# Earlier weights, a first gate one step sooner, and one group's x through GpSimd's queue

## The chip, the cores and the metric

The kernel runs on one core of a Trainium2 chip. The metric is the device time of one execution in microseconds; for each kernel the median of several executions is taken. A profile of one execution gives the instructions of each engine with their times: TensorE (PE, with its weight loads PEld), VectorE (DVE), ScalarE (ACT), GpSimd (POOL) and SyncE (SP), which issues most of the DMA transfers.

## What is computed

A gated linear attention runs over 768 positions for 4 batches of 8 heads (head dimension 48); its output, as 3072 rows of 384, goes through a multiplicative feed-forward network.

```python
for t in range(S):
    state = alpha[:, :, t, :, None] * state + np.einsum('bhd,bhe->bhde', k[:, :, t], v[:, :, t])
    y[:, :, t] = np.einsum('bhd,bhde->bhe', q[:, :, t], state)
x = y.transpose(0, 2, 1, 3).reshape(B * S, H * D)   # 3072 x 384
a = x @ w1                                          # 384 x 1024
b = x @ w2                                          # 384 x 1024
h = a * b @ w3                                      # 1024 x 1024
out = h @ w_out                                     # 1024 x 384
```

The four inputs of the attention are float32. The four weights are float64, and the kernel reads them as pairs of 32-bit words and makes float32 of them itself.

## The kernel before

The attention is cut into 24 chunks of 128 positions, six for each batch, and step n of the loop at L577 deals with chunk n. A step has these parts: `scores(n)` (k times q for each head, L344, masked by VectorE at L347), `transposed(n + 1)` (the next chunk's q and k turned by TensorE, L304, and copied by ScalarE, L306), `attend(n - 1)` (the masked scores times v, L370, with the part that comes from the state, L364, ahead of it in `attend_state`), `outer(n)` (the chunk's own contribution to the state, L316, added by VectorE at L324 or L326), `decayed(n + 2)` (q and k multiplied by their decays, L282), `logs(n + 4)` (L251) and `decays(n + 3)` (sums of logarithms by a matmul, L266 or L269, and two exponentials, L272 and L273).

For every even chunk that isn't the first of its batch, the state has to be scaled by a decay over two chunks. Its factors lie in single rows, across partitions where they are needed along them, so they go through memory: GpSimd's queue stores a row of alpha (L258) and two rows of exponentials (L277, L275) into `ends`, reads them back as columns into `dec` (L290), multiplies them (L333, L334) and scales the state (L335). L335's result is read by VectorE at L326 and by TensorE at L364.

The output of a chunk, x, is copied out of PSUM by ScalarE (L374, two copies) and stored by two DMA transfers into `xd[g]`, where g = n // 3 is the group of three chunks. The transfers are put on the list `later`, and the next step's `store()` (L241) issues them on SP's queue. When a group is complete, `load_x(g)` (L386) loads it as `xT`, and `split_x` splits it into three parts for float32-accurate products: ScalarE takes a rounded part (L392), VectorE two remainders (L393, L394).

The feed-forward network begins inside this loop. `begin` says at which step a group is loaded; two steps later it is split, and its gates (a tile of 128 columns of a and of b) are put on the list `fill`. In each step `run` takes so many pieces from this list as `pieces` says: 0, 3, 3, 2 in turn. A piece is one factor of one tile: nine matmuls at L400, then L409 and L411, and after the second factor the product of the two (L448).

The gates need w1 and w2 in float32. They are converted in twelve units of 128 x 512 elements (`load_gates`). A unit begins with two transfers of 256 KB of raw words (L183); then come four portions of work, one for each call of `convert(1)`: L191, L192, L195 and L196; then L198, L199 and L201; then L209; then L211 and L212. The first six units serve the first four tiles, three units for two tiles each. At most three units are under way at once, and `rawp` has three buffers. `fetch` begins units without doing any of their portions.

On each engine and each queue the instructions run in order. That order isn't always the order of the program: the tile framework orders instructions by its own estimate of when they are ready. What follows the loop (the other gates, w3 folded with w_out, the last projection) is mostly TensorE's work at L400.

Of the kernel before, what the change touches and what calls it, by code (L numbers as in the profile page):

```python
# [48 lines left out]
def kernel(  # L49
# [12 lines left out]
    nc = tc.nc  # L62
    B, H, S, D = q.shape
    C = 128
# [5 lines left out]
    DP = 64  # L70
    KM = DM // C
    KF = DF // C
# [46 lines left out]
    def rows(src, n):  # L119
        b, c = divmod(n, NCH)  # L120
        return src[b, :, ds(c * C, C), :].rearrange("h p d -> p h d")

    def load_a(n):
        if n < N:
            st["a", n] = inp.tile([C, H, D], FP32, tag="ac", name="ac")
            nc.sync.dma_start(out=st["a", n], in_=rows(alpha, n))

    def load_kq(n):
        if n >= N:
            return  # L130
        st["kq", n] = inp.tile([C, 2, H, D], FP32, tag="kq", name="kq")
        nc.sync.dma_start(out=st["kq", n][:, 0], in_=rows(k, n))
        nc.sync.dma_start(out=st["kq", n][:, 1], in_=rows(q, n))

    def load_v(n):
        if n < N:
            st["v", n] = vs[n % len(vs)]
            nc.sync.dma_start(out=st["v", n][:, :, 0:D], in_=rows(v, n))
# [77 lines left out]
    def fetch(ahead=3):  # L216
        while weights and len(begun) < ahead:
            begun.append(weights.popleft())
            next(begun[-1])

    def convert(steps, ahead=3):

        for _ in range(steps):
            fetch(ahead)
            if not begun:
                return
            x = begun.popleft()
            try:
                next(x)
                begun.appendleft(x)  # L230
            except StopIteration:
                pass


    later = deque()

    def store():

        while later:
            dst, src = later.popleft()  # L240
            nc.sync.dma_start(out=dst, in_=src)  # L241
# [18 lines left out]
    def decays(n):  # L260
        if n >= N:
            return
        lc = bank()[:, 0:DM]
        la = st.pop(("la", n))
        if n < LATE:
            nc.tensor.matmul(lc, utri if n % 2 else after, la, start=True, stop=True)  # L266
        else:
            for i in range(2):
                nc.tensor.matmul(lc, sums[:, n % 2], la[:, i], start=(i == 0), stop=(i == 1))  # L269

        e = st["e", n] = work.tile([C, 2, DM], FP32, tag="e", name="e", bufs=3)
        nc.scalar.activation(e[:, 0], lc, AF.Exp, scale=-1.0)  # L272
        nc.scalar.activation(e[:, 1], lc, AF.Exp)  # L273
        if n in ends:
            nc.gpsimd.dma_start(out=ends[n][0:1], in_=e[0:1, 0])  # L275
        if n + 1 in ends:
            nc.gpsimd.dma_start(out=ends[n + 1][1:2], in_=e[C - 1:C, 1])  # L277
        load_ends(n)

    def decayed(n):  # L280
        if n < N:
            nc.vector.tensor_mul(qks[n % 3][:, :, :, 0:D], st.pop(("kq", n)),  # L282
                                 st.pop(("e", n)).rearrange("p i (h d) -> p i h d", h=H))
# [69 lines left out]
    def attend_state(n):  # L353
        qkT = st.pop(("qkT", n))

        y = [bank()[:, 0:HP * C].rearrange("p (j c) -> p j c", c=C) for _ in range(2)]
        st["y", n] = y, [(half * HP + j, i, y[i][ds(DP * half, DP), j, :])
                         for j in range(HP) for i in range(2) for half in range(2)]  # L360
        if n % NCH:
            for j, i, to in st["y", n][1]:
                r = ds(DP * i, D)
                nc.tensor.matmul(to, Ts[n % 2][r, j, :], qkT[r, 1, j, :],  # L364
                                 start=(j % HP == 0), stop=False, skip_group_check=True)

    def attend(n):
        (y, heads), ms, vc = st.pop(("y", n)), st.pop(("ms", n)), st.pop(("v", n))
        for j, i, to in heads:
            nc.tensor.matmul(to, vc[:, 2 * j + i, :], ms[:, i, j, :], start=(n % NCH == 0 and j % HP == 0),  # L370
                             stop=(j % HP == HP - 1), skip_group_check=True)
        x = work.tile([C, HP, 2, C], FP32, tag="x", name="x")
        for i in range(2):
            copied = nc.scalar.copy(x[:, :, i], y[i])  # L374
        ends_of_part1[1] = copied.ins
        x = x.rearrange("p j i t -> p (j i) t")

        g, c = divmod(n, G)
        to = xd[g].rearrange("(b h d) t -> b d h t", b=2, d=D)
        for half in range(2):  # L380
            later.append((to[half, :, :, ds(c * C, C)], x[ds(DP * half, D)]))


    def load_x(g, queue=nc.sync):
        st["xT", g] = xp.tile([C, KM, TG], FP32, tag="xT", name="xT")
        queue.dma_start(out=st["xT", g], in_=xd[g].rearrange("(k p) t -> p k t", p=C))  # L386
# [82 lines left out]
    def gate(g, f):  # L469
        yield from (late_gate if late else early_gate)(g, f)  # L470
# [83 lines left out]
    FH = CW // C  # L554
# [7 lines left out]
    transposed(0)  # L562
    logs(1)
    decays(1)
    convert(1, 1)
    load_v(1)
    load_kq(2)
    load_a(3)
    decayed(1)
    load_v(2)  # L570
    load_kq(3)
    load_a(4)


    begin = {4 + 4 * g: (g, range(FH if g < 4 else KF)) for g in range(5)}

    for n in range(N + 1):  # L577
        store()
        load_v(n + AHEAD - 1)
        load_a(n + 5)  # L580
        load_kq(n + AHEAD)
        if n:
            attend_state(n - 1)
        if n < N:
            scores(n)
        transposed(n + 1)
        if n - 2 in begin:
            g, tiles = begin[n - 2]
            split_x(g, 0)
            fill.extend(gate(g, f) for f in tiles)  # L590
        pieces = (0, 3, 3, 2)[(n - 6) % 4] if n > 5 else 0
        if n == 0:
            logs(2)
            decays(2)
            logs(3)
        early = n < 7
        if n < N - 2:
            convert(1, 2 if n == 0 else 3)
        advance(n)
        if n:  # L600
            attend(n - 1)
        outer(n)
        run(pieces > 0)
        if early:
            convert(1)
        decayed(n + 2)
        logs(n + 4)
        if n in begin:
            load_x(begin[n][0])
        convert(early and n > 2)  # L610
        run(pieces > 1)
        decays(n + 3)
        if n < N - 2:
            convert(early or n % 3 == 0)
        run(pieces > 2)
        if n == N - 3:
            while begun:
                convert(1)
            weights.extend(load_out(j) for j in range(KF))
            fetch()  # L620
# [91 lines left out]
```

## Time and profile before

| | us |
|---|---|
| median of 11 executions | 485.95 |
| lowest and highest | 484.06 and 489.77 |
| the profiled execution | 483.23 |
| its span | 481.4 |
| TensorE, mean granted clock | 0.992 |

The profiled execution is a little faster than the median, and its span, from the first to the last instruction, leaves out 1.8 us around it. All waits and durations below belong to this one execution. A few groups of instructions from the page, with the busy time, the mean duration of one, and the idle time of the engine just before them:

```profile
L400 PE MATMUL bank<-x,w 128*128 128x384 f32 x1152 | 211.1, 338 | 0.4 <-DVE x L394 0.4
L282 DVE TENSOR_TENSOR qk<-kq,e 128x768 f32<-128x768 f32 x24 | 22.9, 952 | 9.4 <-ACT e L273 7.3
L347 DVE TENSOR_TENSOR ms<-bank,keep 128x512 int32<-128x512 int32 x48 | 31.1, 683 | 1.3 <-PE bank L344 1.3
L196 ACT ACTIVATE power<-power,rebias 128x512 uint32<-128x512 uint32 (+1 forms) x36 | 25.1, 698 | 15.6 <-DVE power L195 15.6
```

The durations of matmuls overlap, since they are pipelined: 338 ns is not the distance of one from the next. The same holds, to a smaller degree, for VectorE. The page's DMA issues that matter for the start:

```profile
xT<-xd SPq DMA_DIRECT2D x14, 576.0 KB, 4.2
raw<-in_moe_w_dram SPq DMA_DIRECT2D x24, 256.0 KB, 4.7
xd<-x SPq DMA_DIRECT2D x48, 96.0 KB, 3.9
ends<-e POOLq DMA_DIRECT2D x16, 1.5 KB, 3.7
dec<-ends POOLq DMA_DIRECT2D x16, 2.2 KB, 5.0
```

The last column is the median time from issue to landing.

### The profile page before, as it was taken

The numbers are of one execution on the slowest core, as the hardware profiler recorded it, in microseconds if no ns is written. First come the engines' busy times: TensorE is split into PE (matmuls) and PEld (weight loads), VectorE is DVE, ScalarE is ACT, GpSimd is POOL, SyncE is SP. The second block draws the span as 40 slices with busy tenths as digits, with TensorE's granted clock in tenths as the row PEclk, the third lists the DMA queues.
The fourth block names the chain that finished last, engine by engine and source line by source line (L and its number), as shares of the span: only waits on it lengthen the run. The fifth ranks groups of instructions, "written<-read, shape, count | busy, mean of one in ns | idle before, by whom it ended". The sixth has DMA issues, their size and how long they took to land.

```text
span 481.4 us, 9979 instructions
## 1 busy us (share of the span) xinstructions
PE 452.4 (94%) x3824; PEld 429.9 (89%) x3824; DVE 358.5 (74%) x582; ACT 277.4 (58%) x550; POOL 36.5 (8%) x83
## 2 busy tenths in 40 slices
PE   3779679999998999999999998999999999999997
PEld 1557469899898989999999997999999999999996
DVE  2769899997989676999977896884456366667671
ACT  2667667876767544888765665656446333333330
POOL 2122122112202200000000000000000000000000
PEclk9988999999999999999999999999999999999999
DMA  9989999999999954656773353320219455555511
GB/s 170 190 177 219 215 211 205 230 211 248 186 219 222 215 157 124 204 159 216 238 242 96 112 180 114 100 83 34 98 57 266 143 160 169 170 175 177 180 50 50
DMA packets 161295, 80.29 MB, mean 167 GB/s; under 512 B 104672, under 2 KB 155104, under 8 KB 161248
## 3 DMA queue, kind: packets, MB, share of 16 engines
q1 hardware_dynamic: 159968, 79.58, 65.8%
q8 instruction: 30, 0.49, 0.4%
q0 software_dynamic: 1280, 0.08, 0.4%
q14 instruction: 17, 0.14, 0.1%
HBM read 57.58 MB, written 22.06 MB: 165 GB/s over the span
## 4 chain that ended last, share of the span: by engine, by line
PE 75%; DVE 9%; DMA 7%; ACT 3%; issue 2%; SPq 2%; POOL 0%; DVEq 0%; POOLq 0%; ACTq 0%
PE bank L400 63%; PE bank L344 3%; PE bank L370 3%; DMA raw<-in_moe_w_dram 3%; PE bank L304 1%; PE bank L364 1%; DMA dec<-ends 1%; DVE ms L347 1%; DMA ac<-in_alpha_dram 1%; PE bank L502 1%; DVE qk L282 1%; PE bank L316 1%; DMA xd<-x 1%; DMA ends<-e 1%; DVE x L394 1%
## 5 line engine op out<-in xcount | busy, mean ns | idle before, releaser
L400 PE MATMUL bank<-x,w 128*128 128x384 f32 x1152 | 211.1, 338 | 0.4 <-DVE x L394 0.4
L400 PEld LDWEIGHTS bank<-x,w 128*128 128x128 f32 x1152 | 199.9, 188 | 2.8 <-issue 1.4
L400 PE MATMUL bank<-w3o,ab 128*128 128x384 f32 x576 | 100.2, 336 | 0.0
L400 PEld LDWEIGHTS bank<-w3o,ab 128*128 128x128 f32 x576 | 99.9, 188 | 0.0
L425 ACT ACTIVATE bank<-bank 128x384 f32<-128x384 f32 x98 | 46.7, 478 | 36.0 <-PE bank L400 35.7
L409 ACT ACTIVATE t<-bank 128x384 f32<-128x384 f32 x62 | 30.4, 491 | 63.6 <-PE bank L400 63.4
L461 DVE TENSOR_TENSOR ab<-bank,r 128x384 f32<-128x384 f32 x45 | 24.9, 554 | 23.3 <-ACT bank L425 11.5
L531 DVE TENSOR_TENSOR ab<-abl,ab 128x1024 fp32r<-128x1024 f32 x24 | 29.4, 1224 | 13.5 <-ACT ab L530 13.5
L400 PE MATMUL bank<-wo,w3T 128*128 128x384 f32 x192 | 36.3, 335 | 1.9 <-DVE w3T L505 1.1
L530 ACT ACTIVATE ab<-abl 128x1024 fp32r<-128x1024 f32 x24 | 25.5, 1061 | 20.0 <-PE bank L400 18.8
L400 PEld LDWEIGHTS bank<-wo,w3T 128*128 128x128 f32 x192 | 33.4, 188 | 2.5 <-DVE w3T L505 1.4
L344 PEld LDWEIGHTS bank<-qkT 48*128 48x128 f32 x384 | 25.0, 199 | 10.6 <-ACT qkT L306 3.8
L196 ACT ACTIVATE power<-power,rebias 128x512 uint32<-128x512 uint32 (+1 forms) x36 | 25.1, 698 | 15.6 <-DVE power L195 15.6
L306 ACT COPY qkT<-bank 128x512 f32<-128x512 f32 x48 | 25.9, 586 | 14.0 <-PE bank L304 13.9
L411 DVE SCALAR_TENSOR_TENSOR o<-bank,t 128x384 f32<-128x384 f32 x24 | 13.4, 558 | 27.4 <-issue 15.3
L344 PE MATMUL bank<-qkT 48*128 48x128 f32 x384 | 29.7, 297 | 4.3 <-ACT qkT L306 2.6
L191 ACT ACTIVATE rest<-raw 128x512 f32<-128x512 uint32 (+1 forms) x36 | 23.3, 646 | 16.7 <-DMA raw<-in_moe_w_dram 16.6
L347 DVE TENSOR_TENSOR ms<-bank,keep 128x512 int32<-128x512 int32 x48 | 31.1, 683 | 1.3 <-PE bank L344 1.3
L282 DVE TENSOR_TENSOR qk<-kq,e 128x768 f32<-128x768 f32 x24 | 22.9, 952 | 9.4 <-ACT e L273 7.3
L532 DVE SCALAR_TENSOR_TENSOR ab<-ab,abl 128x1024 fp32r<-128x1024 f32 x24 | 29.2, 1218 | 0.0
L411 DVE SCALAR_TENSOR_TENSOR r<-bank,t 128x384 f32<-128x384 f32 x38 | 21.0, 553 | 10.8 <-PE bank L400 7.1
L370 PE MATMUL bank<-ms,v 128*64 128x128 f32 x384 | 27.1, 285 | 0.0
(73 smaller groups left out, 530.6 us busy)
## 6 DMA issues: line engine op xcount, KB each, us to landing
abd<-ab SPq DMA_DIRECT2D x64, 192.0 KB, 2.7
abl<-abd SPq DMA_DIRECT2D x24, 512.0 KB, 4.6
raw<-in_moe_w_dram SPq DMA_DIRECT2D x16, 512.0 KB, 4.5
xT<-xd SPq DMA_DIRECT2D x14, 576.0 KB, 4.2
raw<-in_moe_w_dram SPq DMA_DIRECT2D x24, 256.0 KB, 4.7
ac<-in_alpha_dram SPq DMA_DIRECT2D x24, 192.0 KB, 5.0
kq<-in_k_dram SPq DMA_DIRECT2D x24, 192.0 KB, 5.0
kq<-in_q_dram SPq DMA_DIRECT2D x24, 192.0 KB, 4.5
```

What stands on the lines that cost most here:

```text
L282: nc.vector.tensor_mul(qks[n % 3][:, :, :, 0:D], st.pop(("kq", n)), st.pop(("e", n)).rearrange("p i (h d) -> p i h d", h=H))
L306: nc.scalar.copy(qkT[:, :, :, ds(DP * half, DP)], tp[half])
L344: nc.tensor.matmul(sc[i][:, j, :], qkT[r, 0, j, :], qkT[r, 1, j, :], start=True, stop=True)
L347: masked = nc.vector.tensor_tensor(ms[:, i].bitcast(I32), sc[i].bitcast(I32), keep_bc, op=ALU.bitwise_and)
L370: nc.tensor.matmul(to, vc[:, 2 * j + i, :], ms[:, i, j, :], start=(n % NCH == 0 and j % HP == 0), stop=(j % HP == HP - 1), skip_group_chec ...
L400: nc.tensor.matmul(p, w[part][i], x[part][i], start=start and part == parts[0] and i == 0, stop=stop and part == parts[-1] and i == n - 1, ...
L409: nc.scalar.activation(t, p1, AF.Copy, scale=(1.0 + 1.0 / P) * scale)
L411: nc.vector.scalar_tensor_tensor(to, p2, scale, t, op0=ALU.mult, op1=ALU.add)
L425: nc.scalar.activation(p, p, AF.Copy, scale=1.0 + 1.0 / P)
L530: nc.scalar.activation(t[:, 0], ab, AF.Copy, scale=1.0 - 2.0 ** -13)
L531: nc.vector.tensor_sub(t[:, 1], ab, t[:, 0].bitcast(FP32))
L532: nc.vector.scalar_tensor_tensor(t[:, 2], t[:, 0].bitcast(FP32), -1.0 - 1.0 / P, ab, op0=ALU.mult, op1=ALU.add)
```

## The change

There are four edits, all of them in the part that runs the attention.

1. Ahead of the loop, the raw words of three units are fetched instead of one, between the input loads of steps 1 to 3, and three portions of the first unit are done instead of one.
2. In the loop, the number of conversion portions in each step is changed: four in each of the steps 0 to 4, then one at step 5, and one or two a step from there on. Before, there were three in each of steps 0 to 2, four in steps 3 to 6, and one or two after that.
3. The stores of x for chunks 0 to 2 (group 0) are issued by GpSimd's queue as soon as the copy is made, instead of by SP's queue at the start of the next step; the load of group 0's xT goes through GpSimd's queue too. All other groups keep SP's queue.
4. Each group's load, split and gates come one step sooner: `begin` starts at 3 instead of 4, and `pieces` is shifted by one step with it.

```diff
@@ attend(n)
         for half in range(2):
-            later.append((to[half, :, :, ds(c * C, C)], x[ds(DP * half, D)]))
+            move = to[half, :, :, ds(c * C, C)], x[ds(DP * half, D)]
+            if g:
+                later.append(move)
+            else:
+                nc.gpsimd.dma_start(out=move[0], in_=move[1])
@@ ahead of the loop
     decays(1)
-    convert(1, 1)
+    fetch(1)
     load_v(1)
+    fetch(2)
     load_kq(2)
     load_a(3)
+    fetch(3)
+    convert(1)
     decayed(1)
+    convert(2)
     load_v(2)
     load_kq(3)
     load_a(4)
-    begin = {4 + 4 * g: (g, range(FH if g < 4 else KF)) for g in range(5)}
+    begin = {3 + 4 * g: (g, range(FH if g < 4 else KF)) for g in range(5)}
@@ in the loop
-        pieces = (0, 3, 3, 2)[(n - 6) % 4] if n > 5 else 0
+        pieces = (0, 3, 3, 2)[(n - 5) % 4] if n > 4 else 0
...
-        early = n < 7
+        early = n < 5
         if n < N - 2:
-            convert(1, 2 if n == 0 else 3)
+            convert(1)
...
         if n in begin:
-            load_x(begin[n][0])
-        convert(early and n > 2)
+            load_x(begin[n][0], nc.gpsimd if n == 3 else nc.sync)
+        convert(early)
         run(pieces > 1)
         decays(n + 3)
         if n < N - 2:
-            convert(early or n % 3 == 0)
+            convert(early or (n > 5 and n % 3 > 0))
         run(pieces > 2)
```

The lines of the changed kernel stand four lower than before from L385 on, and eight lower from the loop's preamble on.

## The prediction

> **What bounds the kernel now.** I read four views: the page's slices, the table of stretches of five microseconds, then GpSimd's and TensorE's instructions in order of time. The page first:
>
> ```profile
> span 481.4 us, 9979 instructions
> PE 452.4 (94%) x3824; PEld 429.9 (89%) x3824; DVE 358.5 (74%) x582; ACT 277.4 (58%) x550; POOL 36.5 (8%) x83
> PE   3779679999998999999999998999999999999997
> POOL 2122122112202200000000000000000000000000
> PEclk9988999999999999999999999999999999999999
> ```
>
> A slice is 12 us. TensorE has gaps in the first six slices alone, so only the start (0 to 70 us) can lose or give time; what follows is TensorE's own work, and moves as a block. The stretches (columns: busy us of PE, PEld, DVE, ACT, POOL, then clock, DMA share, GB/s):
>
> ```profile
> 20.00:25.00 5.00, 4.33 (x69) 3.54 (x68) 4.85 (x8) 4.17 (x11) 1.08 (x3) 1.00 1.44 184
> 25.00:30.00 5.00, 5.00 (x84) 3.66 (x82) 2.93 (x7) 2.73 (x6) 1.79 (x3) 1.00 0.74 205
> 30.00:35.00 5.00, 1.99 (x25) 1.66 (x26) 2.58 (x6) 3.02 (x8) 1.38 (x4) 0.82 1.02 160
> 35.00:40.00 5.00, 5.00 (x61) 4.79 (x58) 4.72 (x10) 3.60 (x7) 1.40 (x2) 0.50 0.88 218
> 40.00:45.00 5.00, 5.00 (x84) 3.78 (x83) 5.00 (x10) 3.51 (x8) 1.45 (x3) 1.00 1.23 221
> ```
>
> From 40 us VectorE is full; between 25 and 35 it is half idle. Why, GpSimd's order shows:
>
> ```profile
> 24.89 1.40 POOL L290 DMA_DIRECT2D dec<-ends  x2 [1.60 <-DMA ends<-e]
> ...
> 31.90 0.20 POOL L333 TENSOR_TENSOR dec<-dec 128x4 f32<-128x4 f32 x1 [5.11 <-DMA dec<-ends]
> 32.18 0.20 POOL L334 TENSOR_TENSOR dec<-dec,dec 128x4 f32<-128x4 f32 x1
> 32.46 0.51 POOL L335 TENSOR_TENSOR T<-tmp,dec 128x192 f32<-128x192 f32 x1
> 32.91 0.53 POOL L275 DMA_DIRECT2D ends<-e  x1
> 37.08 1.40 POOL L290 DMA_DIRECT2D dec<-ends  x2 [3.64 <-DMA ends<-e]
> 42.73 0.75 POOL L333 TENSOR_TENSOR dec<-dec 128x4 f32<-128x4 f32 x1 [4.25 <-DMA dec<-ends]
> 43.55 0.20 POOL L334 TENSOR_TENSOR dec<-dec,dec 128x4 f32<-128x4 f32 x1
> 43.83 0.51 POOL L335 TENSOR_TENSOR T<-tmp,dec 128x192 f32<-128x192 f32 x1
> ```
>
> GpSimd is 8% busy, but it is a queue of round trips: every second step it sends three rows out (L258, L275, L277), waits 4.2 us until they lie in memory, reads them back (5.65 us from 37.08 to 42.73) and scales the state (L335). A busy share of 8% says nothing of how long an instruction waits in that queue. And TensorE:
>
> ```profile
> 33.02 1.06 PE L364 MATMUL bank<-qkT,T 48*64 48x128 f32 x16 [3.01 <-POOL T L335]
> 34.01 2.08 PE L344 MATMUL bank<-qkT 48*128 48x128 f32 x16
> ...
> 63.92 1.31 PE L400 MATMUL bank<-x,w 128*128 128x384 f32 x6
> ...
> 71.08 0.67 PE L364 MATMUL bank<-qkT,T 48*64 48x128 f32 x16
> ```
>
> It waits 3 us for that state, runs at half clock afterwards, and begins the first gate (L400) at 63.92. From L364 of step 8 at 71.08 its instructions follow without a gap, so I compare the two kernels at this instruction.
>
> **What the Trainium skill says.** DMA: Bandwidth & Descriptors, section "Issuing engines are not separate DMA queues": transfers from GpSimd's queue run on the same 16 engines, and only issue time is saved; here each of SP's xd<-x takes a median 0.44 us to issue. The same page, "Latency and other measured facts", has a first byte after about 1 us for GpSimd's descriptors against 0.6 us; the trace has no large transfer from GpSimd, so this stays an estimate. SBUF — State Buffer, the box on the "DVE blocks DMA" trap: VectorE operations in a two-port mode keep GpSimd from writing descriptors. The trace doesn't agree for what GpSimd issues now: L258, L275 and L277 take 0.48 to 0.66 us, full VectorE or not; but its arithmetic stretches (L333 0.19 to 1.29 us). TensorE: Matmul & The Clock Gate, Part 1: half clock after an idle window of about 3.4 us. Agrees: after 3.01 us idle, L344 takes 2.08 us instead of 1.16, and 35 to 40 us has clock 0.50.
>
> **The change part by part.** Lines are those of before.
>
> *Raw words.* Two more units (two transfers of 256 KB each) go on SP's queue, one ahead of kq and alpha of steps 2 and 3, one ahead of the loads after them. SP issues eight input loads from 13.68 to 22.42, 1.09 us each, and four raw ones in 3.85 us from 22.42: 1.9 us a unit. So kq(2) and alpha(3) come 1.9 us later, the loads up to q(4) 3.9 us, and the later ones 1.9 us, as a fourth unit stands ahead of them. q(4), waited for until 27.14 now, comes at about 31. Alpha(3), at about 19.5, is just in time for L251 at 20.11: I take 0.5 us, all of it in the shadow of the round trip of the state, which ends at 31.9. Unhidden it would be 3.9 us.
>
> *Conversions.* Nothing is added; a unit costs VectorE 0.34+0.34+5x0.60 = 3.7 us (L192, L195; L198, L199, L201, L211, L212, by their distances). Units 2 and 3 move from 29–42 us into VectorE's idle time; between 13.1 and 63.9 us its waits sum to 8.7 us (1.0, 1.2, 2.1, 2.4, 0.3, 0.7, 0.7, 0.3). Walking VectorE's new order with these distances, all that stands ahead of x's split (L393) ends at about 50.5 us; there L393 stands behind the mant operation (L198) of unit six. Before, L393 came at 62.86, with one step more done.
>
> *x by GpSimd.* Six stores and the load of xT leave SP and join the queue shown. In the new order the two stores of chunk 0 stand ahead of L275 and L335 of the first round trip, those of chunk 1 ahead of the second L333, those of chunk 2 ahead of the second L335, and the load behind it. A store's issue isn't in the trace: between L258's 0.51 and L290's 0.70 us, I take 0.6. Then: L334 ends 32.4 (as before); L258 to 32.9; stores to 34.1; L275 to 34.6; L335 to 35.2, 2.2 us later than now. The rows land 4.2 us after L275's start at 34.1: 38.3; L290 to 39.7; stores of chunk 1 to 40.9; L333 5.65 us after L290's start, 43.95; products to 45.05 (1.1 us, as 42.73 to 43.83); only then the stores of chunk 2, to 46.2, though x(2) was ready at about 41.6; their landing, 4.0 us after the issue of the second at 45.6, is the median of xd<-x: 49.6. The xT load lands 4.2 us (median now) to 5.2 us after that: 53.9 to 54.9, I take 54.5. ScalarE's split (L392) 1.17 us: 55.7.
>
> So a new wait: ScalarE stands at L392 until 54.5, with L196 of unit six, L251 of step 8 and qkT behind it; VectorE at L393 from 50.5 to 55.7, 5.2 us, with the scores' mask (L347), L394, unit six's end and qk(7) behind it; and TensorE, whose gate stands behind the transposes of qk(7), waits for VectorE. After 55.7: L393 1.27, four operations at 0.60, L394 1.27, L211 and L212 1.2, L282 0.87: 62.7. Then transposes (L304) 0.6 and L316 0.55, and 0.3 for the slow clock after this idle time (at most 1): the first gate at 64.2 us.
>
> *A step sooner.* From there TensorE has, until L364 of step 8: 54 gate matmuls (18 take 3.24 us, from 74.74 to 77.98, so 9.8), L266 0.55, L269 0.35, and one step's L344, L304, L370, L316 at 1.0+0.6+0.93+0.55: 13.8 us. L364 of step 8 at 78.0. But 54 gate matmuls stand before it now and 27 then, 4.9 us of work taken from later, so the same progress before is 71.08+4.9 = 76.0. Balance: +2.0 us, and I add 0.2 us for later x copies. The xd buffers: x(3)'s copy waits for chunk 1's store, landed at 44.9, before L370 of step 3 is done: nothing. Cover gone, a microsecond for each one of lateness.
>
> Forecast: +2.2 us on the span of 481.4 (483.6). The profiled execution was 483.23 us in all, 1.8 us around the span, and lies below the median of the runs; the difference is put on the median: 485.95+2.2 = 488.2.
>
> **The rivals.**
> - *B, faster: VectorE packed, x in time.* If the round trips under GpSimd take what the fastest ones now take (dec 3.8, ends 2.8, xd 2.0, xT 3.8 instead of 5.65, 4.2, 4.0, 4.9), the load is there by 50 and VectorE never waits: the gate comes 5.2 us sooner, -3.0 us: 483.0. It decides from xT landing before about 52.5, where the balance is nil. For: five links, each with a minimum well below its median. Against: they are added, and DMA is fuller in this stretch.
> - *C, no difference:* xT between 51 and 54; also if VectorE is late for other reasons, so that the wait for x takes its place: 486.
> - *D, much slower:* the loads put back are not hidden (3.9 us) and the later first L335 lengthens TensorE's idle time at half clock: 488.2+3.9 = 492. For: q(4) was waited for already. Against: it is now needed at about 36.
> - *E: the step sooner exists in the order only*, the conversions not being ready: about 486 too, counted with C.
>
> **How the numbers follow.** A 0.58 (0.50 slower, 0.08 within the bound), B 0.18 (0.14 faster), C and E 0.12 (0.10 within, 0.02 faster), D 0.12. What a measurement can tell is 0.3%, 1.5 us. Faster 0.16, same 0.22, slower 0.62. The likeliest one's own range is 486.5 to 491. The whole one reaches to B's value and D's: 483.3 to 492.3.
>
> **What would show it.** Right: in the timeline VectorE idle for 3 to 7 us before the subtraction of x's split, released by ScalarE's split, that by the DMA into xT; chunk 2's stores on GpSimd several us after x(2)'s copy; the first L335 near 35; the first gate between 62 and 67 us. Wrong: no wait at the split, or the first gate before 62; a time under 486; or waits for kq and alpha before 30 us (then D).

## The result, and the profile after

The changed kernel takes 490.16 us (median of 12 executions, 488.50 to 492.36), against 486.09 us of the kernel before, measured beside it. The ratio is 1.0089, with a 95% interval of 1.0066 to 1.0112: slower by 3.2 to 5.4 us. The forecast was 488.2. The profiled execution took 488.5 us, its span 486.7, 5.3 us more than the span before.

The page of the changed kernel:

```profile
span 486.7 us, 9983 instructions
PE   3778199999899999999999999999999999999997
POOL 2054112202311220000000000000000000000000
PEclk9999679999999999999999999999999999999999
```

The slice to look at is the fifth of PE, 48.7 to 60.8 us: the digit is 1, where the kernel before had 6. Then the stretches, columns as before (busy us of PE, PEld, DVE, ACT, POOL, then clock, DMA share, GB/s):

```profile
25.00:30.00 5.00, 3.77 (x68) 2.81 (x64) 5.00 (x10) 3.76 (x9) 1.38 (x3) 1.00 1.11 142
30.00:35.00 5.00, 3.88 (x66) 3.14 (x66) 4.97 (x9) 3.60 (x9) 4.40 (x7) 1.00 1.01 224
...
50.00:55.00 5.00, 0.00 (x0) 0.00 (x0) 0.00 (x0) 0.00 (x0) 1.83 (x3) 0.80 0.88 238
55.00:60.00 5.00, 0.52 (x1) 0.50 (x2) 1.57 (x2) 2.77 (x5) 0.00 (x0) 0.50 0.97 199
60.00:65.00 5.00, 5.00 (x42) 3.39 (x42) 5.00 (x8) 3.38 (x8) 0.49 (x1) 0.50 0.88 211
```

VectorE's idle time between 25 and 35 us is gone (5.00 and 4.97 us busy, 2.93 and 2.58 before). From 50 to 55 us TensorE, VectorE and ScalarE do nothing at all. GpSimd's instructions in order of time say what they wait for:

```profile
38.82 1.40 POOL L290 DMA_DIRECT2D dec<-ends  x2 [3.69 <-DMA ends<-e]
40.22 1.17 POOL L385 DMA_DIRECT2D xd<-x  x2
43.84 0.44 POOL L333 TENSOR_TENSOR dec<-dec 128x4 f32<-128x4 f32 x1 [2.45 <-DMA dec<-ends]
44.36 0.20 POOL L334 TENSOR_TENSOR dec<-dec,dec 128x4 f32<-128x4 f32 x1
44.58 1.16 POOL L385 DMA_DIRECT2D xd<-x  x2
45.74 0.52 POOL L335 TENSOR_TENSOR T<-tmp,dec 128x192 f32<-128x192 f32 x1
50.27 0.80 POOL L390 DMA_DIRECT2D xT<-xd  x1 [4.01 <-DMA xd<-x]
```

Chunk 2's stores (the L385 at 44.58) stand behind the wait for dec, and the load of xT (L390) waits 4.01 us for them. It lands at 57.23, 7.0 us after its issue (by the start of ScalarE's split; the tile view says 6.9). ScalarE's, VectorE's and TensorE's instructions in order of time, one line each of where the wait ends, and TensorE's next:

```profile
57.23 1.16 ACT L396 ACTIVATE x<-xT 128x1152 fp32r<-128x1152 f32 x1 [8.77 <-DMA xT<-xd]
```

```profile
58.43 1.36 DVE L397 TENSOR_TENSOR x<-xT,x 128x1152 fp32r<-128x1152 f32 x1 [8.60 <-ACT x L396]
```

```profile
59.48 1.65 PE L266 MATMUL bank<-la,after 128*128 128x384 f32 x2 [9.88 <-ACT la L251]
...
67.50 1.66 PE L404 MATMUL bank<-x,w 128*128 128x384 f32 x8
...
81.46 0.67 PE L364 MATMUL bank<-qkT,T 48*64 48x128 f32 x16
```

TensorE doesn't need x at 49.6 us; it needs the logarithm of alpha (L251), which stands on ScalarE behind x's split. The first gate starts at 67.50 (63.92 before), and L364 of step 8 at 81.46, 5.5 us above the 76.0 at which the two kernels would be level.

### The profile page after: what moved, and what is told of

Same layout as the page of the kernel before. It is cut to its first block, busy times and chain, and to the rows that moved or that the text cites. A ratio compares the mean times of both kernels' runs of the same rounds, so it can differ in the third digit from the quotient of the medians.

```text
span 486.7 us, 9983 instructions
## 1 busy us (share of the span) xinstructions
PE 454.5 (93%) x3824; PEld 431.7 (89%) x3824; DVE 361.9 (74%) x584; ACT 275.0 (57%) x549; POOL 45.3 (9%) x90
## 3 DMA queue, kind: packets, MB, share of 16 engines
q0 software_dynamic: 1712, 1.26, 1.2%
## 4 chain that ended last, share of the span: by engine, by line
PE 76%; DMA 8%; DVE 7%; ACT 3%; issue 2%; SPq 2%; POOL 1%; DVEq 0%; POOLq 0%; ACTq 0%
PE bank L404 65%; PE bank L370 3%; PE bank L344 2%; DMA dec<-ends 2%; DMA ends<-e 2%; PE bank L506 1%; DMA xT<-xd 1%; PE bank L304 1%; DMA xd<-x 1%; DVE ms L347 1%; DMA raw<-in_moe_w_out_dram 1%; PE bank L364 1%; DMA raw<-in_moe_w_dram 1%; PE bank L316 1%; DVE qk L282 1%
## 5 line engine op out<-in xcount | busy, mean ns | idle before, releaser
L413 ACT ACTIVATE t<-bank 128x384 f32<-128x384 f32 x64 | 31.5, 492 | 68.9 <-PE bank L404 68.7
L344 PEld LDWEIGHTS bank<-qkT 48*128 48x128 f32 x384 | 25.8, 204 | 9.6 <-ACT qkT L306 4.2
L196 ACT ACTIVATE power<-power,rebias 128x512 uint32<-128x512 uint32 (+1 forms) x36 | 25.1, 702 | 16.0 <-DVE power L195 15.9
L415 DVE SCALAR_TENSOR_TENSOR r<-bank,t 128x384 f32<-128x384 f32 x40 | 22.2, 554 | 16.1 <-ACT t L413 12.0
L344 PE MATMUL bank<-qkT 48*128 48x128 f32 x384 | 30.6, 304 | 3.2 <-ACT qkT L306 2.8
L282 DVE TENSOR_TENSOR qk<-kq,e 128x768 f32<-128x768 f32 x24 | 23.0, 959 | 7.3 <-ACT e L273 7.3
L370 PE MATMUL bank<-ms,v 128*64 128x128 f32 x384 | 27.1, 285 | 0.0
```

The costliest lines, as they stand in the source:

```text
L344: nc.tensor.matmul(sc[i][:, j, :], qkT[r, 0, j, :], qkT[r, 1, j, :], start=True, stop=True)
L413: nc.scalar.activation(t, p1, AF.Copy, scale=(1.0 + 1.0 / P) * scale)
L415: nc.vector.scalar_tensor_tensor(to, p2, scale, t, op0=ALU.mult, op1=ALU.add)
```

## The experiments

The theory of the prediction: the late x costs all of the loss; the rest of the change would gain. Its rivals: the weights' part is at fault itself; the half clock after the wait is; GpSimd's queue is slow for so large a transfer. The table has all kernels that ran. "Balance" is the start of L364 of step 8 in the trace, less the level at which the kernel would be as fast as the kernel before: 76.0 for kernels whose groups begin a step sooner (the prediction works it out), 71.1 for the others. The loss is the ratio less 1, times 486 us.

| kernel | median us | ratio and interval | first gate | balance | loss |
|---|---|---|---|---|---|
| changed kernel | 490.16 | 1.0089 (1.0066 to 1.0112) | 67.50 | +5.5 | +4.3 |
| e3_q_for_x | 482.05 | 0.9927 (0.9899 to 0.9954) | 59.97 | -2.1 | -3.5 |
| e1_x_by_sp | 486.84 | 1.0025 (1.0002 to 1.0048) | 59.46 | +0.9 | +1.2 |
| e2_x_gpsimd_alone | 494.53 | 1.0189 (1.0154 to 1.0225) | 77.28 | +12.2 | +9.2 |
| e5_weights_alone | 491.20 | 1.0110 (1.0080 to 1.0139) | 67.86 | +6.6 | +5.3 |
| e4_load_by_sp | 488.94 | 1.0080 (1.0056 to 1.0105) | 67.91 | +5.8 | +3.9 |
| e9_hold_loads | 487.63 | 1.0020 (0.9999 to 1.0041) | 65.67 | +3.6 | +1.0 |
| e6_after_filler | 493.04 | 1.0143 (1.0105 to 1.0180) | 67.49 | +6.4 | +6.9 |
| e10_x_by_sp_filler | 486.80 | 1.0015 (0.9990 to 1.0040) | 62.53 | +1.2 | +0.7 |
| e11_x_sooner | 485.71 | 1.0000 (0.9979 to 1.0021) | 63.02 | +1.1 | 0.0 |
| e12_x_sooner_split_behind | 485.88 | 1.0011 (0.9992 to 1.0030) | 61.10 | +0.4 | +0.5 |
| e7_weights_filler | 489.72 | 1.0104 (1.0068 to 1.0140) | 68.03 | +5.7 | +5.0 |
| e8_before_filler | 485.10 | 0.9992 (0.9974 to 1.0010) | 66.46 | +1.9 | -0.4 |

The balance is one execution's and the loss a median's, and the two agree to within 3 us over a spread of 14. So one instruction of the trace carries the result, and each experiment can be read there, to these 3 us. Two things go into them: the profiled execution of the kernel before lies 2.7 us below its median, so that both levels are a little low, and TensorE, which the prediction has going on without a gap, still waits afterwards here and there: 3.6 us in all in the kernel before, 3.0 in the changed one.

**x without its way through memory.** The first group's load takes data of q, which lies in memory from the start, in place of x; it waits for nothing but its place behind chunk 1's stores. Group 0's gates so work on other data; the stores of x are still made.

```diff
-        queue.dma_start(out=st["xT", g], in_=xd[g].rearrange("(k p) t -> p k t", p=C))
+        src = xd[g].rearrange("(k p) t -> p k t", p=C)
+        if g:
+            queue.dma_start(out=st["xT", g], in_=src)
+            return
+        with tc.issue_after(mark["store"]):
+            queue.dma_start(out=st["xT", g], in_=q.rearrange("b h s d -> (b h s d)")[ds(0, DM * TG)].rearrange("(k p t) -> p k t", p=C, t=TG))
...
-            split_x(g, 0)
+            with tc.issue_after(mark[n + 2]):
+                split_x(g, 0)
```

`mark` holds chunk 1's second store and each step's second exponential (L273); the lines that fill it are left out here.

> The changed kernel, but the load of group 0's x takes a piece of q of the same size and row length in place of x (so the gates of group 0 compute with other data), and stands on GpSimd's queue right behind the stores of chunk 1; the order on VectorE, ScalarE and TensorE is the same, the stores of x stay. Theory X (the loss is the wait for x, which GpSimd's queue delivers late): the load lands at about 48 us, VectorE's 8.6 us of waiting ahead of the split and TensorE's half clock after it go, the first gate comes at about 58 us, and the time falls to 480 to 484 us, below the kernel before. Rival Y (the loss comes from the raw words ahead of the input loads and from the conversions crowded into steps 0 to 4): no more than 2 us gained, 488 us or more.

It took 482.05 us, 3.5 us less than the kernel before and some 8 less than the changed one. Up to the first gate every engine but GpSimd has the changed kernel's order. Of the split on ScalarE:

```profile
L403 ACT ACTIVATE x<-xT x1: 1166/1166/1166, 50.3 to 50.3; 128x1152 fp32r<-128x1152 f32 x1
```

This is the tile view (durations in ns, then the first and last start): the split begins at 50.3 in place of 57.23. So the wait for x is worth the whole loss and more, and the rest of the change gains where x is in time. (The load's own traffic moves too, to 40.5 to 46.5 us; what that is worth was not separated.)

**x by SP's queue.** The first group's stores, right after the copy, and its load on SP.

```diff
-                nc.gpsimd.dma_start(out=move[0], in_=move[1])
+                nc.sync.dma_start(out=move[0], in_=move[1])
...
-            load_x(begin[n][0], nc.gpsimd if n == 3 else nc.sync)
+            load_x(begin[n][0])
```

> The changed kernel with group 0's stores and load of x on SP's queue, issued at the same places of the program (the stores right after the copy). Theory X: the stores no longer stand behind GpSimd's round trip, which brings the load forward by about 3 us; but SP's queue is full of input loads, so VectorE still waits some 4 us: 485 to 488 us. Rival Y: 489 to 491, as the changed kernel.

It took 486.84 us, as expected. The scheduler put the split later here, and both engines hardly waited for it. ScalarE's line:

```profile
58.25 1.16 ACT L396 ACTIVATE x<-xT 128x1152 fp32r<-128x1152 f32 x1 [0.46 <-DMA xT<-xd]
```

But xT, issued at 51.55, landed at 58.25, 6.7 us after: by SP's queue it isn't fast either. (Since the order is another one, this run says nothing of the queue alone; e4_load_by_sp below does.)

**x by GpSimd's queue, without the rest.** The kernel before with its first group's stores and load on GpSimd.

```diff
-            later.append((to[half, :, :, ds(c * C, C)], x[ds(DP * half, D)]))
+            move = to[half, :, :, ds(c * C, C)], x[ds(DP * half, D)]
+            if g:
+                later.append(move)
+            else:
+                nc.gpsimd.dma_start(out=move[0], in_=move[1])
...
-            load_x(begin[n][0])
+            load_x(begin[n][0], nc.gpsimd if n == 4 else nc.sync)
```

> The kernel before with group 0's stores and load of x through GpSimd's queue, nothing else (load at step 4, as before). Theory X: the stores of chunk 0 put the state's scaling 1.2 us later, and the load, 7 us from GpSimd's queue, lands at about 61 us where ScalarE's split came at 60.2: 1 to 2 us slower than before, 487 to 488.5. Rival Y: 486, no difference.

It took 494.53 us, 6 us more than expected. The scheduler places by estimates of its own, and it put x's split on ScalarE 17 instructions ahead of where it stands in the kernel before. ScalarE by time:

```profile
58.28 1.16 ACT L396 ACTIVATE x<-xT 128x1152 fp32r<-128x1152 f32 x1 [8.20 <-DMA xT<-xd]
59.35 0.51 ACT L251 ACTIVATE la<-ac 128x384 f32<-128x384 f32 x1
```

x landed 2 us sooner than in the kernel before (58.28 against 60.2), and yet ScalarE, TensorE and VectorE stood for 7.6 to 8.2 us. It isn't the landing that costs here, but what is queued behind the instruction that waits for it: L251, which TensorE needs, and L196, which VectorE needs. How much of the 9.2 us that is, and how much the rest of the new order, this run doesn't tell.

**The weights' part without the rest.** The changed kernel with x as before: by SP, groups beginning at step 4.

```diff
-            if g:
-                later.append(move)
-            else:
-                nc.gpsimd.dma_start(out=move[0], in_=move[1])
+            later.append(move)
...
-    begin = {3 + 4 * g: (g, range(FH if g < 4 else KF)) for g in range(5)}
+    begin = {4 + 4 * g: (g, range(FH if g < 4 else KF)) for g in range(5)}
...
-        pieces = (0, 3, 3, 2)[(n - 5) % 4] if n > 4 else 0
+        pieces = (0, 3, 3, 2)[(n - 6) % 4] if n > 5 else 0
...
-            load_x(begin[n][0], nc.gpsimd if n == 3 else nc.sync)
+            load_x(begin[n][0])
```

> The changed kernel's raw words and conversion portions alone: x of all groups by SP's queue, groups begin at steps 4, 8 and so on as before. Theory X: VectorE's idle time before 35 us is filled with units 2 and 3, so that all that stands ahead of x's split is done some 4 us sooner and the first gate comes at 59 to 61 us: 482 to 484.5. Rival Y: the crowded start costs 1 to 4 us: 487 to 490.

It took 491.2 us: my theory expected 482 to 484.5 and was wrong by 7 us. VectorE's instructions by time around x's split (L394 here, L393 before), of this kernel and then of the kernel before:

```profile
66.60 0.68 DVE L198 SCALAR_TENSOR_TENSOR mant<-mant,rest 128x512 f32<-128x512 uint32 x1
67.85 0.36 DVE L326 TENSOR_TENSOR tmp<-bank,T 128x192 f32<-128x192 f32 x1 [0.57 <-PE bank L316]
68.13 1.35 DVE L394 TENSOR_TENSOR x<-xT,x 128x1152 fp32r<-128x1152 f32 x1
```

```profile
62.86 1.35 DVE L393 TENSOR_TENSOR x<-xT,x 128x1152 fp32r<-128x1152 f32 x1
```

The split comes 5.3 us later, at the same step, though VectorE's waits between 10 and 75 us are no longer than before (11.9 against 12.4 us). It has more work in front: the order of its instructions has 90 ahead of this one, and 79 before. The eleven are two each of L192, L195 and L198, one each of L199, L201, L211, L212 and L326. By their distances (0.34, 0.34 and 0.60 us for the first three, 0.60 for the next four, 0.27 for the last) that is 4x0.34 + 6x0.60 + 0.27 = 5.2 us. The first tiles need six units, and this is work on the seventh and eighth. So conversions spread sooner, with the groups where they were, push work that isn't due yet in front of the first gate. With the groups a step sooner and x in time they were part of a gain (e3_q_for_x). The step sooner without the conversions was not run.

TensorE also ran at half clock in this kernel (0.66 from 50 to 60 us), which could have been the cause. For that, matmuls whose result nobody reads were put into TensorE's waits. In this and all kernels below, the order of every engine's other instructions is held to that of the kernel they start from, by edges that fix only the order of issue. The edit, with its bookkeeping left out:

```diff
+    def warm(k, behind):
...
+        idle = bank()[:, 0:C]
+        with tc.issue_after(behind):
+            for _ in range(k):
+                mark["warm"] = nc.tensor.matmul(idle, utri, ident, start=True, stop=True).ins
...
             scores(n)
+            warm({3: 3, 4: 5, 5: 3, 6: 5, 7: 6}.get(n, 0), mark["scores"])
...
         outer(n)
+            warm({5: 13, 6: 4}.get(n, 0), mark["end"])
```

> The kernel e5_weights_alone (conversions of weights as in the changed kernel, x as before; 491.2 us, where 482 to 484.5 was expected) with 39 matmuls of 128x128 that nobody reads in TensorE's waits of steps 3 to 7, the order of all else held. Clock theory of its loss: TensorE, waiting for VectorE here and there, fell to half clock from 40 us on, and VectorE waited for it (2.68 us for L344, 0.66 for L316). With the clock full: L344 at 55 takes 1.16 us and not 2.08, the first gate starts at 64.5 to 66.5 (67.86 now), its 18 matmuls take 3.4 to 4 us and not 7.5, L364 of step 8 comes at 72.5 to 75 (77.71) and the time is 485.5 to 488.5. Order theory: the order that the scheduler makes of the spread conversions is what costs, and the clock only follows: 489.5 to 492.

It took 489.72 us, and the ratios of the two kernels (1.0110 and 1.0104) can't be told apart. One stretch of this kernel, with the clock after the five busy times:

```profile
50.00:60.00 10.00, 10.00 (x136) 8.75 (x133) 6.09 (x11) 5.08 (x12) 1.85 (x4) 1.00 0.94 222
```

The clock is full (TensorE busy all of 50 to 60 us), L344 takes 1.16 us, and the split still starts at 68.01, the first gate at 68.03. The half clock of e5_weights_alone cost nothing that this measurement can tell.

**The half clock of the changed kernel.** 44 such matmuls in its wait from 49.6 us on (`warm(44, ...)` behind step 5's last matmul).

> The changed kernel with 44 matmuls of 128x128 whose result nobody reads, put on TensorE where it waits from 49.6 to 59.48 us for the logarithm (L251) that stands behind x's split on ScalarE; the order of everything else is held. They take some 8.3 us and should keep the clock full. In the changed kernel L266 to L316 after the wait took 8.0 us, 3.3 us of it for the half clock (L266 1.65 for 0.91, L364 1.13 for 0.67, L344 2.08 for 1.16, L370 1.97 for 1.09). VectorE theory: its chain behind the split (L282 ends at 65.53 and releases L304) sets the first gate, so that the half clock costs only L304 and L316 their 0.5 us: first gate 66.8 to 67.2, time 489 to 490.2. Clock theory: most of the 3.3 us is on the path: first gate 64.5 to 66, time 486.5 to 488.5.

TensorE by time:

```profile
61.08 1.16 PE L344 MATMUL bank<-qkT 48*128 48x128 f32 x16
62.17 1.09 PE L370 MATMUL bank<-ms,v 128*64 128x128 f32 x16
65.70 0.83 PE L304 MATMUL bank<-ident,qk 64*128 64x64 f32 x16 [2.44 <-DVE qk L282]
66.47 1.09 PE L316 MATMUL bank<-v,qk 128*64 128x48 f32 x16
67.49 4.35 PE L404 MATMUL bank<-x,w 128*128 128x384 f32 x18
```

The changed kernel at the same place, TensorE's lines and then VectorE's:

```profile
64.12 1.97 PE L370 MATMUL bank<-ms,v 128*64 128x128 f32 x16
66.03 0.94 PE L304 MATMUL bank<-ident,qk 64*128 64x64 f32 x16
```

```profile
64.58 0.95 DVE L282 TENSOR_TENSOR qk<-kq,e 128x768 f32<-128x768 f32 x1
```

L344 and L370 ran at full rate, and TensorE then waited 2.44 us for VectorE's L282; x landed at the same time as in the changed kernel (57.27). The first gate starts at 67.49 (67.50 without these matmuls). So most of the 3.3 us is not on the path to the gate; VectorE's work behind the split is. Not quite all: in the changed kernel TensorE came to L304 only at 66.03, 0.5 us after L282's end, since L370 was still running. Here it came at 65.70, but in the wait of 2.44 us the clock dropped again, and L304 and L316 took 1.79 us where they had taken 1.47. Neither theory's figures came: the VectorE theory had the gate at 66.8 to 67.2. The time went up, to 493.04: 0.9 us of it is there at L364 of step 8, since the lower clock now fell into the gate (4.35 us for 18 matmuls that take 3.4 at full rate). Of the remaining 2 us of the median I don't know the cause.

In the kernel with x by SP, the 18 matmuls of the first gate took 6.93 us; 12 matmuls went into the wait of 2.51 us ahead of them. The line of e1_x_by_sp:

```profile
59.46 6.93 PE L404 MATMUL bank<-x,w 128*128 128x384 f32 x18 [2.51 <-ACT x L396]
```

> The kernel e1_x_by_sp (the changed kernel with the first group's stores and load on SP's queue; 486.84 us) with 12 matmuls of 128x128 that nobody reads on TensorE in its wait of 2.51 us ahead of the first gate; the order of everything else is held. In e1_x_by_sp the 18 matmuls of the first gate took 6.93 us from 59.46, against 3.4 us of the same 18 later, and L364 of step 8 came at 76.85. Clock theory: the gate matmuls take 3.4 to 3.8 us, L364 of step 8 comes at 73 to 74, and the time is 483 to 484.5, faster than both kernels. If the matmuls are slow for another reason (they wait for x's third part or for weights), they stay at 6 to 7 us and the time at 486 to 487.5.

486.80 us: no change. The 18 took 1.30 and 2.34 us in two pieces and so ran at full rate, but from 62.53 on; what follows them, L266, starts at 66.43 (66.19 without the fillers). In this execution the clock was halved earlier, from L304 at 55.40 on, and VectorE waited 2.18 us for L316. xT also came 1.5 us later (59.71). The half clock had moved and not gone, so this run doesn't decide what it costs there.

The kernel before with 14 such matmuls meant for its wait of 3.01 us at 30 to 33:

> The kernel before with 14 matmuls of 128x128 that nobody reads on TensorE in its wait of 3.01 us for the state (30.0 to 33.0), the order of all else held. In the kernel before, L364 to L266 after this wait run at half clock and take 7.7 us for 4.9 of work. Clock theory: VectorE has idle time there, so TensorE sets the pace and up to 2.5 us of it come through: 483 to 484.8. Pace theory: from 40 us on VectorE is full and its work, not TensorE's, sets the first gate: within 1.5 us of the kernel before.

485.10 us. It doesn't test that wait: the matmuls came at 37.1, behind the step after it, where TensorE didn't wait. In the profiled execution the wait was 1.11 us by itself, and L364 behind it took 0.67 us, the full rate; still the first gate came at 66.46, no sooner than 63.92.

**Why xT took 7.0 us.** One instruction moved: xT's load from GpSimd's queue to SP's, between the raw words and v.

```diff
-            load_x(begin[n][0], nc.gpsimd if n == 3 else nc.sync)
+            load_x(begin[n][0])
```

> The changed kernel with one instruction moved: the first group's xT load is issued by SP (behind the raw words that it issues at 47.3 us, ahead of v) in place of GpSimd; the six stores stay on GpSimd, and the order of every engine is held to that of the changed kernel. Two theories of why xT took 7.0 us from issue to landing and not the 4.2 to 5.2 predicted. Traffic: the kq, alpha, v and raw loads beside it fill the DMA engines, whoever issues it. Then it still lands 6 to 7 us after its issue, the first gate (L404) starts at 67 to 67.8 us and the time is 489.5 to 491. Route: a large transfer from GpSimd's queue is slow. Then it lands 4.2 to 5.2 us after, the first gate starts 2 to 2.7 us sooner, and the time is 487.3 to 488.3.

```profile
51.32 0.38 SPq L390 DMA_DIRECT2D xT<-xd  x1
```

```profile
57.19 1.16 ACT L396 ACTIVATE x<-xT 128x1152 fp32r<-128x1152 f32 x1 [8.40 <-DMA xT<-xd]
```

Issued by SP at 51.32 (DMA queue's instructions by time), landed at 57.19 (ScalarE's): 5.9 us, a little under what the traffic theory said and over the other one's 4.2 to 5.2. It lands at the same instant as by GpSimd, and the ratio, 1.0080, can't be told from the changed kernel's (the median, 488.94, lies between the two theories'). That instant is the finding: with SP's loads in place xT landed at 57.23 (changed kernel), 57.19 (here) and 57.27 (e6_after_filler), though it was issued at 50.27, 51.32 and 49.57. Over these 1.8 us its own issue didn't set it. Next, xT on GpSimd again, and SP's later loads kept back until it has landed: a store of 64 bytes that reads xT stands ahead of them.

```diff
             load_x(begin[n][0], nc.gpsimd if n == 3 else nc.sync)
+            if n == 3:
+                seen = dram.tile([1, 16], FP32, name="seen")
+                mark["seen"] = nc.sync.dma_start(out=seen, in_=st["xT", 0][0:1, 0, 0:16]).ins
```

> The changed kernel with a 64-byte store of a piece of xT put into SP's queue where SP stands at 49.9 us, so that v, alpha, kq and raw, which SP issues between 49.95 and 57.8 us, are issued only when xT has landed; xT itself still comes by GpSimd, and the order of every engine is held. Traffic: xT lands 3.5 to 4.9 us after its issue (7.0 now), the first gate starts at 64.5 to 65.8 us in place of 67.5 and the time is 487 to 488.8, unless the loads held back are late in their turn, which would give it back from 70 us on. Route: still 6.5 to 7.5 us, and 490 or more.

The tile view of xT, its last line the time from issue to landing:

```profile
L390 POOL DMA_DIRECT2D xT<-xd x1: 796/796/796, 50.9 to 50.9; - x1
...
L396 ACT ACTIVATE x<-xT x1: 1162/1162/1162, 55.3 to 55.3; 128x1152 fp32r<-128x1152 f32 x1
...
DMA to landing us min/median/max: 4.4/4.4/4.4
```

4.4 us in place of 7.0, by the same queue. The first gate came at 65.67, L364 of step 8 at 79.62, and the loss fell from 4.3 to 1.0 us. So the excess came from the traffic beside it: v, alpha, k and q, 192 KB each, and 512 KB of raw words, which SP issues from 49.95 us on.

**x still sooner.** Chunk 2's two stores ahead of L333 in GpSimd's queue, and SP's loads kept back from 47.3 us on: the same store of 64 bytes, two places earlier in SP's order.

> The changed kernel with x's way shortened at two places, the order of all else held: the two stores of chunk 2 stand ahead of the products L333 and L334 in GpSimd's queue (GpSimd waits there until 43.84 us anyway), and SP issues nothing of its later loads (raw words, v, alpha, kq) between 47.3 us and the landing of xT. If the wait for x is all that the change lost: stores issued by 42.9 in place of 45.7, in memory at 47.3, load landed 4.4 us later at 51.7 (57.2 now), first gate at 62, L364 of step 8 at about 76, and 484 to 485.7, no longer slower than before. If the loads held back, or another wait, take the place: L364 of step 8 after 78.5 and 487 or more.

TensorE by time:

```profile
63.02 3.54 PE L404 MATMUL bank<-x,w 128*128 128x384 f32 x18
...
77.12 0.67 PE L364 MATMUL bank<-qkT,T 48*64 48x128 f32 x16
```

The load was issued at 46.2 (50.27 in the changed kernel) and landed at 52.2 (57.23): 6.0 us after the issue this time. k and q were in flight beside it (issued at 43.33 and 46.01), but that this is the reason is not shown: in e9_hold_loads the raw words had been issued just ahead, from 48.74 us on, and it took 4.4. The chain can be followed step by step against the changed kernel: issue 4.1 us sooner, landing 5.1, first gate 4.5, L364 of step 8 4.3, loss 4.3 (485.71 us). Each point came about 1 us later than expected; at a ratio of 1.0000 (0.9979 to 1.0021) the loss is gone.

Then x's split behind the work of the next step that doesn't need x: on ScalarE behind six instructions, among them L251, for which TensorE had waited; on VectorE behind four. In shorthand, by the order of the lines:

```diff
 ScalarE: ... L272 L273
-         L396
          L196 L251 L306 L306 L374 L374
+         L396
 VectorE: ... L198
-         L397 L199 L347 L201 L347 L398
+         L199 L201 L347 L347 L397 L398
```

> As e11_x_sooner, and x's split stands later on two engines, so that nothing is queued behind the wait that doesn't need x: on ScalarE behind L196, L251, the copies to qkT and x's copies of the next step; on VectorE its subtraction stands behind L199, L201 and the two masks of the next step. x then arrives at 51.7 before either engine reaches the split (51.9 and 53.1): no wait of over 1 us for x, the first gate at 59 to 60.5 us, L364 of step 8 at 73 to 74.5, and 481.5 to 483.5, faster than both kernels. If VectorE alone sets the pace, it gains 1 us or less over e11_x_sooner.

485.88 us, not the 481.5 to 483.5 hoped for; the other outcome that was written down, 1 us or less, is what came. TensorE by time:

```profile
50.55 0.91 PE L266 MATMUL bank<-la,after 128*128 128x384 f32 x2 [1.26 <-ACT la L251]
...
59.02 1.12 PE L304 MATMUL bank<-ident,qk 64*128 64x64 f32 x16 [4.85 <-DVE qk L282]
...
61.10 4.78 PE L404 MATMUL bank<-x,w 128*128 128x384 f32 x18
```

TensorE's wait of 9.88 us has become one of 1.26 and one of 4.85. xT was late again (6.6 us from issue to landing), VectorE waited 1.75 us for it, and then had its row of work to do before L282. The first gate came 1.9 us sooner than with the split in front, but its 18 matmuls took 4.78 us in place of 3.54, at a lower clock behind the wait; so L364 of step 8 came only 0.7 us sooner, and the median didn't move. Here, where the gate itself is TensorE's next work, the clock is on the path. No kernel that computes the reference was faster than the kernel before by more than its interval.

## Why the prediction was right, and where its size was off

The mechanism is the one forecast: x comes late through GpSimd's queue, the engines stand behind its split, and the rest of the change would gain. With data that lay in memory from the start the same order took 482.05 us (e3_q_for_x), and with x's way shortened the loss was gone (e11_x_sooner). What was off is the size: +4.1 us in the median for +2.2. In the trace, for which it was worked out, it was off by more, +5.5 for +2.2 (the balance of +2.0 and 0.2 for x's copies); that the medians differ by less was not forecast, and it brought the number nearer. Two of the prediction's own signs were passed: VectorE stood for 8.60 us (3 to 7), and the first gate came at 67.50 (62 to 67).

- *GpSimd's queue.* First L335 forecast to end at 35.2, ended 35.13; second L333 43.95, came at 43.84; chunk 2's stores forecast 45.05 to 46.2, were issued 44.58 to 45.74; the pair 1.2 us, took 1.16 to 1.23. Right, and at the second L333 by two errors that cancel: L290 came 0.5 us later than forecast (38.82 for 38.3), and the way back took 5.0 us for 5.65. x(2)'s copies had ended at 40.99, so its stores stood for 3.6 us.
- *GpSimd's issues.* That they don't stretch beside a full VectorE was read as a disagreement. The traces don't show in which mode VectorE's operations run, so they neither agree nor disagree.
- *The store's landing.* Forecast 4.0 us after the second issue, at 49.6; the load could go at 50.27, 0.7 us late. The second store was issued 0.4 us sooner than forecast (45.16 for 45.6), so its landing took 5.1 us and not 4.0.
- *The load's landing.* "The xT load lands 4.2 us (median now) to 5.2 us after that": the term that failed. 4.9 were taken and it took 7.0, and xT came at 57.23 in place of 54.5. 4.2 is the median of 14 loads, of which this is the first; the first one's own row, in the tile view of the kernel before, had 5.6 us:

```profile
L386 SPq DMA_DIRECT2D xT<-xd x1: 2168/2168/2168, 54.6 to 54.6; - x1
...
DMA to landing us min/median/max: 5.6/5.6/5.6
```

  That was the row to take, though it would still have been 1.4 us short. e9_hold_loads shows what the 7.0 is made of: 4.4 us without the loads that SP issues behind. With the loads held, the median was about what had been forecast: 487.63 against 488.2.

- *The route.* The Trainium skill's page DMA: Bandwidth & Descriptors, section "Issuing engines are not separate DMA queues", says that transfers run on the same engines and interleave, whoever starts them. The runs agree: the first group's xT took 5.2 to 6.7 us by SP and 4.4 to 7.7 by GpSimd, and the two runs that changed one thing each (e4_load_by_sp, e9_hold_loads) put it down to what else was in flight. What exactly delays it stays open in part: 6.0 and 6.6 us in e11_x_sooner and e12_x_sooner_split_behind, with nothing issued by SP behind it.
- *VectorE at the split.* Forecast at 50.5, reached at 49.8. The wait forecast at 5.2 us was 8.60. The work behind it was forecast at 7.0 us (L393 to L282), and took 7.1 (58.43 to 65.53).
- *Half clock.* 0.3 us, at most 1, for the first gate. From L282's end to the first gate it took 2.0 us where 1.15 was worked out: 0.8 us, of which 0.3 is L304 and L316 at the lower rate, as allowed, and 0.5 is L370, which TensorE was still at. Inside the bound. That it isn't the whole 3.3 us has a reason, that VectorE's chain is the longer one; e6_after_filler shows that, where TensorE waits 2.44 us for VectorE.
- *First gate and balance.* Gate 67.50 for 64.2; from there to L364 of step 8 13.96 us for 13.8; balance +5.5 for +2.0. The 3.5 us are xT's landing (2.7: 0.7 from the store, 2.1 from the load), the clock behind the wait (0.5 to 0.6) and the gates (0.2).
- *The step sooner.* That it takes 4.9 us of gates from later was argued, and is borne out: with 76.0 as the level, balances and losses of kernels of both kinds lie in one row, to the 3 us named above.
- *The rivals.* B had the right price for a timely x: 483.0 forecast, 482.05 with q's data. C's value came when x was hurried (485.71), at a landing of 52.2, inside the 51 to 54 named. D, the input loads put back, didn't happen: between 12 and 50 us neither VectorE nor ScalarE has a wait for kq or alpha. (The whole range was to reach to B's value, 483.0, and is given from 483.3.)

What I expected of e2_x_gpsimd_alone and e5_weights_alone was wrong for one reason: I changed one edit at a time and took the rest of the order as given. The scheduler gave e2_x_gpsimd_alone another order, and in e5_weights_alone the spread conversions stood in front of the first gate. The parts don't add: +9.2 and +5.3 alone, +4.3 together with the step sooner.

## What to carry to other kernels

For a transfer's time, take the row of that transfer in its own stretch, and not the median of its like in quieter ones. Even that row can be short where the change gives the transfer other company: it had 5.6 us, and the load took 7.0. So see what else is issued beside it, and whether that can be issued later. Where an instruction will wait, what is queued behind it on its engine waits too, and the engines that need this: 9.88 us of TensorE here, for one logarithm behind a split. But to free what is queued pays only until another engine's work sets the pace: with the logarithm freed (e12_x_sooner_split_behind), L364 of step 8 came 0.7 us sooner and the median stayed. Work moved forward into idle time gains only if what it precedes begins sooner too; otherwise it stands in front of something that is due.

## What the runs showed of the hardware

- The same 576 KB load, issued between 46 and 57 us, took from 4.4 (e9_hold_loads) to 7.7 us (e6_after_filler) from issue to landing. With SP's loads in place it landed at 57.19 to 57.27 whether issued at 49.57, 50.27 or 51.32. Keeping back what SP issues behind it is not all: in e11_x_sooner and e12_x_sooner_split_behind it took 6.0 and 6.6 us, with k and q in flight from before.
- Whether a short wait of TensorE halves its clock is not fixed. Behind a wait of 1.25 us for L282 near 126 us, the changed kernel went on at full rate (L370 1.09 us) and e6_after_filler at half (1.98 us). The Trainium skill's page TensorE: Matmul & The Clock Gate, Part 1, has a free-running activity window, and warns that the number of slow matmuls varies from run to run; this pair agrees. It gives some 3.4 us of idleness for the clock to drop; in e6_after_filler it dropped behind this one gap of 1.25 us, and in the kernel before behind one of 3.01, which the prediction counted as agreement.
- Matmuls put in to keep the clock up moved the first gate no further forward where VectorE set the pace (67.50 to 67.49 in e6_after_filler, 67.86 to 68.03 in e7_weights_filler), and in one kernel of four (e6_after_filler) the median rose by 2.9 us. Inside the gate, TensorE's own work, a lower clock did cost: 4.35 and 4.78 us for 18 matmuls of 3.4 to 3.5.
